# Top-k attention with a mixture of depths: moving half a mask between two rows of maxima, and one-hot slots to GpSimd at the end

## The chip, the cores and the metric

The kernel runs on one core of a Trainium2 chip. The metric is the device time in microseconds (us), the median of several executions. The core's engines run at the same time, each through its own instruction queue in order: TensorE (PE, with its weight loads as PEld), VectorE (DVE), ScalarE (ACT), GpSimd (POOL) and SyncE (SP), which only issues DMAs here. They wait for one another through semaphores.

## What is computed

Two blocks follow each other. The attention block has 8 batches, 8 heads, 576 tokens and a head size of 64. Of every row of scores the 32 largest are kept:

```python
scores = scale * np.matmul(q, k.transpose(0, 1, 3, 2))
kth = np.partition(scores, -top_k, axis=-1)[..., -top_k:-top_k + 1]
mask = scores >= kth
scores = np.where(mask, scores, -1000000000.0)
attn = softmax(scores)            # written out in the original
attn_out = np.matmul(attn, v)
```

The heads are joined to x of shape (8, 576, 512). The second block, the mixture of depths, lets only 128 tokens of each batch through a small network and adds the result to these rows:

```python
scores = np.einsum('bsd,d->bs', x, w_gate)
out = x.copy()
for b in range(B):
    top_idx = np.argpartition(-scores[b], capacity)[:capacity]
    xe = x[b, top_idx]
    ye = np.maximum(xe @ w1, 0.0) @ w2
    g = 1.0 / (1.0 + np.exp(-scores[b, top_idx]))
    out[b, top_idx] = x[b, top_idx] + g[:, None] * ye
```

## The kernel before

**Units and steps.** The scores of a batch are cut into 18 units of two tiles of 128 rows by 576 columns, 144 units in all (`units`). A software pipeline runs over them: one step `n` of the main loop works on several units at once. In step n
- TensorE turns (transposes) the scores of unit n-4 into PSUM and subtracts a large number where the mask says "less than the 32nd" (`weigh`, tiles `ptr`, `less`), multiplies the scores of unit n+1 (`multiply`, tile `ps`), and multiplies the weights of unit n-4 with v (`values`, tile `av`),
- ScalarE takes the exponential of the turned scores (`pT`, `last`), makes one tile's half of the mask of unit n-3 (`less`), copies the scores of unit n+1 out of PSUM (`sc`), copies the values (`xs`), and finds on which side of a bound the scores of unit n-1 lie (`seen`, `sides`),
- VectorE finds a bound for unit n (`find_bound`: eight maxima of 72 columns for each of the two tiles, `cand<-sc`, then three rounds of `best`), and the 32nd largest of unit n-2 (`find_kth`, `next<-y`),
- GpSimd makes the other tile's half of the mask of unit n-3 (`less`), and multiplies scores and sides of unit n-1 (`y<-sc,sides` twice, then the small `y<-steps,seen`).

**The order.** Each engine's order is the order in which the program writes its instructions; nothing rearranges them. Work that may come a little later is kept in lists: `vector_late` holds closures for VectorE, and `flush_vector` runs them. `find_bound` runs them at line 387, that is between the eight maxima of its first tile and those of its second.

**The mixture of depths** of batch b runs as a generator (`mixture`) within the next steps, a part at a time, at the steps that `mix_at` lists: gates, ranks, one-hot slots (`pick`), a matmul that gathers each slot's row number (`multiply_places`), an indirect DMA that gathers the rows (`fetch_rows`), TensorE's parts of the network (`h_ps`, eight parts, and `y_ps`, eight parts), and an indirect DMA that adds the result to the output (`add_rows`, the scatter), which GpSimd issues. In the step in which GpSimd issues a scatter it has no room for its half of the mask, and VectorE makes it: these are the six `scatter_steps`, one for each of the batches 0 to 5 (line 992, used in line 1091). There `mask_of(n - 3, (act, dve))` writes VectorE's half at the top of the step, ahead of the maxima of `find_bound`.

**The end.** Behind the last unit, `closing` (line 736) does the last batch's mixture of depths with nothing left to hide it, while the batch before has its last eight parts of y (`between`) still to do. `count` ranks the tokens; since the last 64 gates come late, the rank is the sum of a count among the first 512 (`ranks`) and one among the last 64 (`others`), and a slot's one-hot row is `slot - rank == others`. Then follow: five matmuls of `multiply_places`, the sum of the parts (`place`), the row numbers (`row_i`), the gather of `xe` by an indirect DMA, four transposes, 32 matmuls of h in four groups (`ps`, `av`, `h_ps`, `ptr`), eight of y into `ps`, one product on VectorE (`gy`), and the indirect DMA that puts the rows (`put_rows`).

Of the line numbers in the profile, L43 stands for almost everything: the helper `InOrder` records every operation there. The groups are told apart by their tiles.

Of the kernel before, what the change touches and what calls it, by code (L numbers as in the profile page):

```python
# [11 lines left out]
ALU = mybir.AluOpType  # L12
# [34 lines left out]
def kernel(  # L47
# [117 lines left out]
    def load_weights():  # L165
        sp.dma_start(
            out=wg, in_=dataclasses.replace(moe_w_gate, ap=[[0, P], [1, HD]])
        )
        sp.dma_start(out=w1, in_=moe_w1.rearrange("(c p) f -> p c f", p=P))
        sp.dma_start(out=w2, in_=moe_w2.rearrange("(c p) n -> p c n", p=P))  # L170

    pe, dve, act, pool, sp = (
        InOrder(tc, e)
        for e in (nc.tensor, nc.vector, nc.scalar, nc.gpsimd, nc.sync)
    )


    late, vector_late, pool_late = [], [], []
# [23 lines left out]
    def room_for_qkv(b):  # L202

        kT = kqpool.tile([P, NHP, R + S], FP32, name="kT")
        qT = kqpool.tile([P, NHP, S], FP32, name="qT")
        return kT, qT, vbufs[b % 2]
# [96 lines left out]
    def turn_pair(rows, hp):  # L306
        tr = ps_tr.tile([P, 2, J, P], FP32, name="ptr")
        for w in range(2):
            rows.turn(2 * hp + w, tr[:, w, :, :])
        for w in range(2):  # L310
            rows.keep(2 * hp + w, tr[:, w, :, :])
# [8 lines left out]
    def load_v(vb, vs):  # L320
        vt, vpair = vs
        v_rows = vb[:, JP:S, :].rearrange("h p d -> p h d")
        for hh in range(2):
            sp.dma_start(
                out=vpair[hh * R : (hh + 1) * R, :, hh, 0:D], in_=v_rows[:, hh::2, :]
            )
        for h in range(H):
            sp.dma_start(
                out=vt[:, h, :, 0:D],
                in_=vb[h, 0:JP, :].rearrange("(p j) d -> p j d", j=J),  # L330
            )
# [109 lines left out]

    def mask(sc, next8, on=None):

        less = wkpool.tile([P, 2, S], BF16, name="less")
        for i, engine in enumerate(on or (act, pool)):
            kth = next8[:, i, 7:8]
            if engine is act:
                act.activation(less[:, i, :], sc[:, i, :], AF.Relu, bias=kth, scale=-1.0)
            else:
                engine.tensor_scalar(  # L450
                    out=less[:, i, :],
                    in0=sc[:, i, :],
                    scalar1=kth,
                    scalar2=None,
                    op0=ALU.is_lt,
                )
        return less

    def turn_some(tr, z, less):
# [7 lines left out]
    def room_to_turn():  # L467
        return ps_tr.tile([P, 2, J, P], FP32, name="ptr"), ps_av.tile(
            [P, 512], FP32, name="av"
        )  # L470
# [62 lines left out]
    def normalise(b, t, xs):  # L533
        n = R if t == J else P
        den = sums[0:n, b * NT + t, :]
        divide(n, xs, of_batch[b][0][0:n, t, :], den)
# [199 lines left out]
    def closing(b, pg, between):  # L736
# [44 lines left out]
        yield  # L781
        spread(J, NT)
        split(*pg)
        for _ in range(3):
            next(between)
        for t in range(J):
            count(t, slice(JP, S), others)
        for t in range(J):
            dve.tensor_scalar(
                out=pick[:, t, :],  # L790
                in0=slot,
                scalar1=rank[:, t : t + 1],
                scalar2=others[:, t : t + 1],
                op0=ALU.subtract,
                op1=ALU.is_equal,
            )
        count(J, slice(0, S), rank)
        dve.tensor_scalar(
            out=pick[0:R, J, :],
            in0=slot[0:R, :],  # L800
            scalar1=rank[0:R, J:NT],
            scalar2=None,
            op0=ALU.is_equal,
# [44 lines left out]
        for fc in range(NFC):  # L848
# [6 lines left out]
            out=gy, in0=ps, scalar=g[:, 0:1], in1=xe, op0=ALU.mult, op1=ALU.add  # L855
# [15 lines left out]
    def split(gate, parts):  # L871

        rest = modpool.tile([P, NT], FP32, name="rest")
        pool.tensor_copy(out=parts[:, :, 1, 0], in_=gate)
        pool.tensor_tensor(rest, gate, parts[:, :, 1, 0], ALU.subtract)
        pool.tensor_copy(out=parts[:, :, 1, 1], in_=rest)
        pool.tensor_tensor(rest, rest, parts[:, :, 1, 1], ALU.subtract)
        pool.tensor_copy(out=parts[:, :, 1, 2], in_=rest)
# [65 lines left out]
    def gates(b, t):  # L944
        dot_tile(t, *of_batch[b])
# [42 lines left out]
    for b in range(B - 1):  # L988
# [3 lines left out]
    scatter_steps = {  # L992
        (b + 1) * per_batch + mix_at_of.get(b, mix_at)[-1] + 1 for b in range(B - 2)
    }

    place_steps = {}
    for b in range(B - 1):
        n = (b + 1) * per_batch + mix_at_of.get(b, mix_at)[6]
# [17 lines left out]
    def is_unit(n):  # L1016
        return 0 <= n < N
# [31 lines left out]
    def mask_of(n, on=None):  # L1049
        b, i = divmod(n, per_batch)  # L1050
        masks[n] = mask(scs[n], next8s[b][:, i, :, :], on)
        if i == per_batch - 1:
            at = 2 * per_batch * b
            pool.tensor_copy(
                out=seen[:, 1, at : at + 2 * per_batch].rearrange("p (n i) -> p n i", i=2),
                in_=next8s.pop(b)[:, :, :, 7],
            )

    for n in range(-1, N):
        b, i = divmod(n, per_batch)  # L1060
        if i == 0 and 0 <= b < B - 1:
            qkv[b + 1] = room_for_qkv(b + 1)
            loading = chain(
                loading, Rows(k[b + 1], q[b + 1], *qkv[b + 1][0:2]).parts()
            )
        if 0 < n + 1 < NHP:
            turn_pair(first_rows, n + 1)
        if n == 1:
            load_v(v[0], qkv[0][2])
        if n == NHP:  # L1070
            load_weights()


        gating = normalised
        if inverting is not None:
            normalised = inverting[0:2]
            vector_late.insert(0, lambda a=inverting: normalise(*a))
            inverting = None
        else:
            normalised = None  # L1080
        if gating is not None:
            vector_late.append(lambda a=gating: gates(*a))

        if is_unit(n - 4):
            tr, av = room_to_turn()
            pT, last, exp = weigh(scs.pop(n - 4), tr, av, masks.pop(n - 4))
            exp()
        if is_unit(n - 3):  # L1090
            mask_of(n - 3, (act, dve) if n in scatter_steps else None)
        flush()
        if is_unit(n + 1):
            b, t, g = units[n + 1]
            ps = room_for_scores()
            multiply(t, g, *qkv[b][0:2], ps)
            b, i = divmod(n, per_batch)
            loads = list(islice(loading, first_loads[i] if b == 0 else loads_at[i]))
            halves = [ps[:, a, :, HALF : HALF + P] for a in range(2)]
            for load, half in zip(loads, halves):  # L1100
                load[0](half)
            scs[n + 1] = keep(ps)
            for load, half in zip(loads, halves):
                load[1](half)
        if is_unit(n - 4):
            b4, t4, g4 = units[n - 4]
            values(t4, g4, pT, last, av, qkv[b4][2])
            if n in place_steps:
                values_bank[0] = av
                next(mixtures[place_steps[n]])  # L1110
            if g4 == 0:
                xs = xpool.tile([P, H, DE], FP32, name="xs")
                if t4 == 0:
                    x = xpool.tile([P, NT, HD], FP32, name="x")
                    pg = gates_of[b4 % 2]
                    of_batch[b4] = x, pg
            keep_values(t4, g4, av, xs)
            if g4 == groups(t4) - 1:
                inverting = b4, t4, xs
                n4 = R if t4 == J else P  # L1120
                keep_sums(n4, xs, sums[0:n4, b4 * NT + t4, :])
            while kept:
                kept.pop(0)()


        if is_unit(n):
            bests[n] = find_bound(scs[n])
        flush_vector()
        flush_pool()
        if is_unit(n - 2):  # L1130
            kth_of(n - 2)
        while after_kth:
            after_kth.pop(0)()


        if is_unit(n - 1):
            what_is_below(n - 1)

        if gating is not None:
            b, t = gating  # L1140
            if t == J:
                store(out[b], of_batch[b][0])
                mixtures[b] = mixture(float(b * S), of_batch[b][1], ranks[:, b, :])
        for b in mix_steps.get(n, ()):
            next(mixtures[b], None)
        b, i = divmod(n, per_batch)
        if i == v_at and 0 <= b < B - 1:
            load_v(v[b + 1], qkv[b + 1][2])
# [72 lines left out]
    for what, op, than, limit in (  # L1221
# [10 lines left out]
            out=sure, in0=far, scalar=limit, in1=sure, op0=than, op1=ALU.mult  # L1232
# [134 lines left out]
```

## Time and profile before

The time before is 854.24 us, the median of 3 runs (853.79 to 854.92). The profiled execution took 852.91 us and spans 851.1 us.

| engine | busy us | share of the span | instructions |
|---|---|---|---|
| PE | 791.2 | 93% | 9839 |
| DVE | 806.8 | 95% | 4904 |
| ACT | 761.2 | 89% | 1704 |
| POOL | 727.5 | 85% | 727 |

All four engines are busy nearly all of the time up to about 800 us. A step takes about 5.5 us. The last 50 us are different: one chain after another of short instructions, in which engines wait for each other. A busy time includes whatever an instruction spends on waiting inside itself, for a port for example, so a high share alone doesn't say which engine sets the pace. A matmul's end is modelled, so that TensorE's shares are rather too high.

### The profile page before, as it was taken

To read this page: it belongs to the slowest core of one execution; us is meant where nothing else is said; L and a number is where in the kernel's file an instruction comes from. 1 tells how busy PE (TensorE), PEld (TensorE's weight loads), DVE (VectorE), ACT (ScalarE), POOL (GpSimd) and SP (SyncE) were. 2 spreads that over 40 slices of the span, in tenths; PEclk is the share of its full clock that TensorE was granted. 3 is DMA by queue.
4 is the path that set the end of the run, shared out by engine and by line. 5 is a ranking of instruction groups with operands and counts; after the bars stand their busy time and mean duration, and the time that the engine had idled before them with its cause. 6 is when DMAs were issued, how large, how long until landed. Compare 5 with 4: busy or idle time off the path is not lost. (4 is left out here: it accounts for less than half of the span.)

```text
span 851.1 us, 28068 instructions
## 1 busy us (share of the span) xinstructions
PE 791.2 (93%) x9839; PEld 610.5 (72%) x9839; DVE 806.8 (95%) x4904; ACT 761.2 (89%) x1704; POOL 727.5 (85%) x727
## 2 busy tenths in 40 slices
PE   5798889988999999999999999999999999999977
PEld 4566667666777778877787777877787777777845
DVE  5999999999999999999999999999999999999960
ACT  4899999999999999999999999999999999989830
POOL 3799889999989989999899999999898998988820
PEclk9899999999999999999999999999999999999998
DMA  9931112321141221511233221412215102101021
GB/s 173 277 71 31 36 64 39 90 50 29 57 96 27 51 39 57 109 40 39 76 54 75 48 44 57 97 27 52 39 57 109 27 6 72 22 15 15 2 70 28
DMA packets 122133, 50.37 MB, mean 59 GB/s; under 512 B 116416, under 2 KB 116416, under 8 KB 120960
## 3 DMA queue, kind: packets, MB, share of 16 engines
q1 hardware_dynamic: 118672, 43.91, 21.5%
q0 software_dynamic: 1728, 4.20, 2.7%
q8 instruction: 79, 1.29, 0.7%
q14 instruction: 70, 0.57, 0.3%
q10 hardware_dynamic: 1584, 0.39, 0.2%
HBM read 36.93 MB, written 11.55 MB: 57 GB/s over the span
## 5 line engine op out<-in xcount | busy, mean ns | idle before, releaser
L43 POOL TENSOR_TENSOR y<-sc,sides 128x576 f32<-128x576 f32 x288 | 365.4, 1290 | 76.8 <-ACT sides L43 74.1
L43 DVE MAX8 cand<-sc 128x8 f32<-128x72 f32 x2304 | 330.3, 216 | 8.4 <-ACT sc L43 8.4
L43 POOL TENSOR_SCALAR less<-sc,next 128x576 bf16<-128x576 f32 x135 | 232.8, 1724 | 5.2 <-DVE next L43 4.5
L43 ACT ACTIVATE sides<-sc,seen 128x576 bf16<-128x576 f32 x288 | 221.0, 768 | 5.2
L43 PE MATMUL ptr<-out_of_reach,less 128*128 128x128 bf16 x1136 | 204.1, 220 | 17.3 <-POOL less L43 17.2
L43 PE MATMUL ptr<-ident,sc 128*128 128x128 f32 x1136 | 213.7, 279 | 0.0
L43 DVE MAX8 next<-y 128x8 f32<-128x584 f32 x288 | 204.4, 751 | 2.2 <-POOL y L43 2.0
L43 PE MATMUL ps<-kT,qT 64*128 64x288 f32 (+1 forms) x1280 | 181.0, 430 | 7.2 <-ACT qT L43 5.3
L43 PEld LDWEIGHTS av<-v,pT 128*64 128x64 f32 x4544 | 144.1, 137 | 49.0 <-ACT last L43 36.6
L43 PE MATMUL av<-v,pT 128*64 128x65 f32 x4544 | 163.8, 224 | 16.4 <-ACT last L43 15.2
L43 PEld LDWEIGHTS ptr<-ident,sc 128*128 128x128 f32 x1136 | 160.4, 141 | 22.3 <-PE av L43 8.7
L43 ACT COPY sc<-ps 128x1152 f32<-128x1152 f32 x144 | 161.0, 1118 | 8.9 <-PE ps L43 7.6
L43 PEld LDWEIGHTS <-less 128*128 128x128 bf16 x1296 | 133.0, 103 | 37.6 <-POOL less L43 23.3
L43 ACT ACTIVATE pT<-ptr 128x1024 f32<-128x1024 f32 x142 | 144.2, 1015 | 16.2 <-PE ptr L43 13.5
L43 DVE MAX8 best<-cand 128x8 f32<-128x24 f32 (+2 forms) x864 | 141.8, 200 | 0.6 <-DVE cand L43 0.6
L43 PEld LDWEIGHTS ps<-kT,qT 64*128 64x128 f32 (+1 forms) x1280 | 98.1, 177 | 45.8 <-issue 21.9
L43 ACT ACTIVATE less<-sc,next 128x576 bf16<-128x576 f32 x143 | 110.6, 774 | 8.9 <-DVE next L43 8.7
L43 DVE MATCH_REPLACE8 cand<-best,cand 128x24 f32<-128x24 f32 (+1 forms) x576 | 101.9, 185 | 0.0
L43 PE MATMUL av<-vpair,last 128*128 128x130 f32 (+1 forms) x314 | 68.1, 317 | 0.0
L43 PE MATMUL h_ps<-xeT,w 128*128 128x128 f32 x464 | 61.9, 278 | 0.2 <-ACT xeT L43 0.2
L43 PEld LDWEIGHTS h_ps<-xeT,w 128*128 128x128 f32 x464 | 56.0, 192 | 2.5 <-ACT xeT L43 1.3
L43 PE MATMUL y_ps<-w,hT 128*128 128x512 f32 x112 | 56.7, 601 | 0.0
(124 smaller groups left out, 865.2 us busy)
## 6 DMA issues: line engine op xcount, KB each, us to landing
v<-in_v_dram SPq DMA_DIRECT2D x64, 128.0 KB, 3.3
out_dram<-x SPq DMA_DIRECT2D x8, 1024.0 KB, 3.9
rows<-in_k_dram SPq DMA_DIRECT2D x56, 128.0 KB, 3.7
rows<-in_q_dram SPq DMA_DIRECT2D x56, 128.0 KB, 3.3
w<-in_moe_w_dram SPq DMA_DIRECT2D x2, 2048.0 KB
gate_row<-row_dram SPq DMA_DIRECT2D x7, 288.0 KB, 4.2
w<-in_k_dram SPq DMA_DIRECT2D x8, 128.0 KB
last<-in_k_dram SPq DMA_DIRECT2D x8, 128.0 KB, 3.1
```

The source lines that it names most:

```text
L43: return lambda *a, **kw: self._tc.keep_in_program_order(fn(*a, **kw))
```

## The change

Two things are changed.

1. In the six scatter steps VectorE's half of the mask is no longer written at the top of the step. `mask` puts it at the head of `vector_late`, and so it runs in `find_bound` between the eight maxima of the first tile and those of the second.
2. In `closing`, three of the four full tiles of one-hot slots that were made by VectorE are made by GpSimd, and one more part of the earlier batch's y is left for the time behind `multiply_places`, in which the gather is under way: two parts come before it and four after it (three and three before the change). The first two of the eight parts come earlier, and are the same in both.

```diff
         for i, engine in enumerate(on or (act, pool)):
             kth = next8[:, i, 7:8]
             if engine is act:
                 act.activation(less[:, i, :], sc[:, i, :], AF.Relu, bias=kth, scale=-1.0)
             else:
-                engine.tensor_scalar(
-                    out=less[:, i, :],
-                    in0=sc[:, i, :],
-                    scalar1=kth,
-                    scalar2=None,
-                    op0=ALU.is_lt,
-                )
+
+                def is_less(engine=engine, i=i, kth=kth):
+                    (engine or dve).tensor_scalar(
+                        out=less[:, i, :],
+                        in0=sc[:, i, :],
+                        scalar1=kth,
+                        scalar2=None,
+                        op0=ALU.is_lt,
+                    )
+
+                if engine:
+                    is_less()
+                else:
+                    vector_late.insert(0, is_less)
         return less
...
-        for _ in range(3):
+        for _ in range(2):
             next(between)
         for t in range(J):
             count(t, slice(JP, S), others)
         for t in range(J):
-            dve.tensor_scalar(
+            (pool if t < 3 else dve).tensor_scalar(
                 out=pick[:, t, :],
                 in0=slot,
                 scalar1=rank[:, t : t + 1],
...
         if is_unit(n - 3):
-            mask_of(n - 3, (act, dve) if n in scatter_steps else None)
+            mask_of(n - 3, (act, None) if n in scatter_steps else None)
```

The first part is there because VectorE's mask and GpSimd's products meet in that step; the second shortens what VectorE has to do before the gather of the end, and gives TensorE more to do while the gather runs.

## The prediction

> **What bounds the kernel now.** I first cut the span into stages with the view of busy time by stretch (columns: stretch, its length, busy time and instructions of PE, PEld, DVE, ACT and POOL, then the granted TensorE clock, the DMA share and GB/s).
>
> ```profile
> 302.00:324.00 22.00, 19.98 (x274) 16.35 (x272) 21.89 (x127) 21.04 (x50) 19.80 (x19) 1.00 0.32 86
> 324.00:401.00 77.00, 76.98 (x958) 58.88 (x957) 76.89 (x483) 74.06 (x167) 71.06 (x70) 1.00 0.24 51
> 401.00:423.00 22.00, 19.97 (x274) 16.34 (x272) 21.89 (x126) 21.04 (x48) 19.73 (x20) 1.00 0.32 85
> ```
>
> A batch takes 99.2 us (its scatter steps begin at 304.1 and 403.3). VectorE has hardly any idle time in either stretch (0.11 us). TensorE has none in the 77 us, and 2.0 us in the 22 us around a scatter. So two chains are tight: VectorE by itself, and TensorE with ScalarE. Next I read the timeline around one scatter, engine by engine (start, us, engine, instruction, idle time before it and its releaser).
>
> ```profile
> 303.17 2.52 POOL L43 TENSOR_TENSOR y<-sc,sides 128x576 f32<-128x576 f32 x2
> 305.64 0.44 POOL L43 TENSOR_TENSOR y<-steps,seen 128x16 f32<-128x16 f32 x1
> 306.42 1.63 POOL L43 DMA_INDIRECT out_dram<-gy,row_i  x1 [0.34 <-DVE less L43]
> ...
> 304.09 1.92 DVE L43 TENSOR_SCALAR less<-sc,next 128x576 bf16<-128x576 f32 x1
> 305.94 2.24 DVE L43 MAX8 cand<-sc 128x8 f32<-128x72 f32 x16
> ...
> 310.29 0.78 ACT L43 ACTIVATE less<-sc,next 128x576 bf16<-128x576 f32 x1 [0.49 <-DVE next L43]
> ...
> 309.85 1.15 PE L43 MATMUL av<-v,pT 128*64 128x65 f32 x32 [0.64 <-ACT last L43]
> 315.96 1.15 PE L43 MATMUL av<-v,pT 128*64 128x65 f32 x32 [0.97 <-ACT last L43]
> ```
>
> ```profile
> 809.87 0.52 DVE L43 TENSOR_SCALAR less<-sc,next 128x576 bf16<-128x576 f32 x1
> ```
>
> The same mask takes 0.52 us at 809.87, beside an almost idle GpSimd, and 1.92 us here. It starts 0.92 us into GpSimd's two products and ends 0.3 us behind them: it stands still while they run. Behind it, `next` of this step is late, and ScalarE waits 0.49 us for that.
>
> Last, the end, from the timeline of TensorE and VectorE and from the instructions of `pick` (ns: least, median, most).
>
> ```profile
> 823.15 0.28 DVE L43 TENSOR_SCALAR pick<-slot,ranks 64x128 bf16<-64x128 f32 x1
> ...
> 823.49 0.17 PE L43 MATMUL av<-parts,pick 64*128 64x6 bf16 x1 [0.81 <-DVE pick L43]
> 823.59 2.84 PE L43 MATMUL y_ps<-w,hT 128*128 128x512 f32 x6
> 827.92 0.63 PE L43 MATMUL ptr<-ident,xe 128*128 128x128 f32 x4 [1.49 <-DMA xe<-out_dram,row_i]
> 829.23 2.86 PE L43 MATMUL ps<-xeT,w 128*128 128x128 f32 x16 [0.56 <-ACT xeT L43]
> 831.88 2.81 PE L43 MATMUL av<-xeT,w 128*128 128x128 f32 x16
> 834.53 1.95 PE L43 MATMUL h_ps<-xeT,w 128*128 128x128 f32 x16
> ```
>
> ```profile
> L43 POOL TENSOR_SCALAR pick<-slot,ranks x28: 599/611/622, 163.8 to 751.9; 128x128 bf16<-128x128 f32 x21, 64x128 bf16<-64x128 f32 x7
> L43 DVE TENSOR_SCALAR pick<-slot,ranks,others x4: 342/343/343, 821.3 to 822.1; 128x128 bf16<-128x128 f32 x4
> ```
>
> The chain is: last `pick` on VectorE, matmul, row numbers, gather, transposes, h. The first two groups of h take 2.8 us, the third 1.95 us for the same work: by the view of stretches the granted clock is 0.50 from about 830.3 to 833.7 us and 1.00 elsewhere.
>
> **What the Trainium skill says.** *SBUF — State Buffer*, section "SBUF: two separate sides": VectorE and GpSimd share a pair of ports as an exclusive lock; a VectorE instruction in a 2-port mode or GpSimd holds it, and the other blocks. The trace agrees (1.92 against 0.52 us), and shows more: the mask didn't get in between the two products. *VectorE: DVE Perf Modes*, section "The perf-mode tier table": a fp32 `tensor_scalar` from SBUF runs at 2x. The durations agree for one operation: between 128 and 576 columns (277 and 508 ns in the trace) a column costs 0.52 ns. The two-operation `pick` takes 342 ns, more than the 277 of one operation, so I take it as running at half that speed, and thus without the lock. *TensorE: Matmul & The Clock Gate*, Part 1: a free-running window of 3.41 us, after a quiet one the clock is halved. The trace agrees: 3.4 us at 0.50.
>
> **Part 1, the masks.** GpSimd's order doesn't change. VectorE does eight maxima first. Sixteen take 2.24 us, so eight take about 1.08 to the next start; the mask is then ready at 304.09 + 1.0 = 305.1, still ahead of the point where it was let in (306.01 - 0.52 = 305.49). It ends at about 306.0 as before, and only eight maxima are left in place of sixteen: VectorE is 1.08 us ahead. The eight maxima take the place of waiting. Behind the mask stand the second tile's maxima, which nobody is waiting for at once; TensorE wants this half at about 311.7, 5.7 us later; GpSimd's scatter sees the mask end when it did. Five of the six masks are alike (1.92 to 1.97 us). The sixth starts at 766.13 and takes 0.81 us; 1.0 later it would meet the scatter's issue, of 1.62 us, which can begin at about 766.9. If nothing blocks it, it ends at 767.6 with eight maxima fewer to do, 0.4 us won; if it stands for the whole issue, it ends at 769.0, and 1.0 us is lost. VectorE has by then a lead, so I count 0.
>
> What is the lead worth? VectorE alone: 5 x 1.08 = 5.4 us, the upper end. The other chain: in the 22 us of a scatter, TensorE's wait of 0.64 us is for ScalarE, busy without a break since 303.1; it stays. The 0.49 us that ScalarE waits for VectorE goes, and with it that much of the 0.97 us in which TensorE waits for ScalarE. From 316 us on TensorE is full for the rest of the batch. So a batch is 0.5 us shorter: 5 x 0.5 = 2.5 us. The rest of the lead, 0.58 us each time, collects as slack on VectorE, for which the scores lie ready 2.4 us or more ahead in most steps. In the last batches ScalarE waits again for VectorE (1.28 us at 754.7, 0.47 at 760.2), and TensorE then 0.76 for ScalarE at 771.2; the slack takes away about 0.6 of that. Part 1: 2.5 + 0.6 = 3.1 us.
>
> **Part 2, the slots.** VectorE loses three instructions of 0.26 us start to start (1.11 for four): its last `pick` is due at 823.15 - 0.77 = 822.38. GpSimd is free at 820.81 (the end of `split`). Before doesn't show it at a `pick` of two operations; at least it costs 0.61 us (one operation), and at most I take 0.9. VectorE's own ratio, 342 to 277, gives 0.75; I take 0.70. Three end at 820.88 + 2.1 = 822.98. VectorE's last `pick` has one operation and so wants the lock: let in 0.2 us before GpSimd's end as the mask was, at 822.78, it ends at 823.06, 0.37 us before 823.43. The gather follows this, so 0.4 us are won (0.6 with 0.61 us, 0.2 lost with 0.9). TensorE does two parts of y before, and idles a little for the slots.
>
> The fourth part behind the slots is 0.86 us (two matmuls of 0.43 start to start). From 823.66 to 827.92 TensorE waits for the gather, 4.26 us; four parts take 2.84 + 0.86 = 3.70, so the part costs nothing, and the gap falls from 1.49 to about 0.6 us. Then comes the clock. The quiet window before was 826.85 to 830.27: 1.07 + 0.56 = 1.63 us idle. The window from 816.6 to 820.0 has 1.53 us idle (from 818.06 to 819.59) and was followed by a full clock. With 0.6 + 0.56 = 1.2 us no window is as quiet as that, so I expect the full clock. Two groups of h then take 3.57 us in place of 5.30 start to start: 1.7 us won. Sum: 3.1 + 0.4 + 1.7 = 5.2 us, 854.2 - 5.2 = **849.0 us**.
>
> **The rivals.**
> - *VectorE is the only bound*: then its lead counts whole, 5.4 + 0.4 + 1.7 = 7.5 us, 846.7 us. For it: no idle time on VectorE in a batch. Against it: none on TensorE in 77 us of it either.
> - *The clock drops all the same*, or the timed runs of before didn't have it low, since the window runs free: 3.1 + 0.4 = 3.5 us, 850.7 us; with only the 0.5 us per scatter and nothing from the slots, 851.7.
> - *Slower*: the mask, coming later, misses its turn, and waits through the small product and the scatter's issue. 306.08 + 1.63 + 0.5 = 308.2 in place of 306.0, less the 1.08 won: 1.1 us lost six times, less 1.7 from the clock: about 859 us. Against it: the mask is waiting 0.4 us before its turn in five of six steps. A weaker form is the slots on GpSimd holding the last `pick` back and the sixth mask held (0.2 + 1.0 lost), with the clock low as before and less than half of the 2.5 us won: about 854, no change.
>
> **How the numbers follow.** My forecast 0.5; VectorE alone 0.2; no clock 0.2; no change or slower 0.1, about half of it each. The range takes the first three with the ends of the unknown costs: 846.2 (846.7 less 0.2 for cheaper slots and 0.3 of the sixth mask's 0.4) to 851.9 (851.7 and 0.2 for dearer slots). Faster by over 0.2% means below 852.5: 0.90; within 0.2%: 0.05; slower: 0.05.
>
> **What would show it.** Right: five masks of about 0.9 us in place of 1.92, with eight maxima ahead of each; no wait of ScalarE's `less` for `next` behind a scatter; the distance from scatter to scatter 0.5 us shorter (1.1 for the first rival); the first two groups of h near 1.95 us at a clock of 1.00; the gap before `ptr<-ident,xe` near 0.6. Wrong: masks that still take 1.9 us; a `pick` on GpSimd over 0.85 us, or VectorE's last `pick` stretched beyond 0.7; a clock of 0.50 within the last 25 us before the final y.

## The result, and the profile after

The changed kernel takes 848.55 us, the median of 6 runs (845.32 to 849.89); the kernel before, run beside it, 853.64 (6 runs, 852.79 to 854.92). The ratio is 0.9933, with an interval from 0.9913 to 0.9954. The forecast was 849.0 us. The profiled executions span 851.1 and 847.1 us. From the page after, each engine's busy time:

```profile
PE 791.5 (93%) x9839; PEld 609.8 (72%) x9839; DVE 803.8 (95%) x4901; ACT 760.2 (90%) x1704; POOL 729.4 (86%) x730
```

VectorE's busy time is 3.0 us shorter. The three slots that left it are 1.0 of that (3 x 342 ns); its other work is the same, so it stands 2 us less inside its instructions. The view of stretches around the first scatter, with the columns of before:

```profile
300.00:322.00 22.00, 20.66 (x272) 16.39 (x268) 22.00 (x137) 21.54 (x51) 20.30 (x20) 1.00 0.23 50
322.00:398.00 76.00, 75.84 (x958) 58.66 (x957) 75.89 (x469) 73.02 (x166) 70.02 (x69) 1.00 0.29 62
```

TensorE now idles 1.34 us around the scatter, where it idled 2.0, and 0.16 us in the rest of the batch. VectorE is still full. The timeline of that scatter step, engine by engine:

```profile
305.27 1.16 DVE L43 MAX8 cand<-sc 128x8 f32<-128x72 f32 x8
306.35 1.04 DVE L43 TENSOR_SCALAR less<-sc,next 128x576 bf16<-128x576 f32 x1
307.30 1.16 DVE L43 MAX8 cand<-sc 128x8 f32<-128x72 f32 x8
...
304.53 2.53 POOL L43 TENSOR_TENSOR y<-sc,sides 128x576 f32<-128x576 f32 x2
...
307.76 1.63 POOL L43 DMA_INDIRECT out_dram<-gy,row_i  x1 [0.31 <-DVE less L43]
...
311.07 0.77 ACT L43 ACTIVATE less<-sc,next 128x576 bf16<-128x576 f32 x1
...
311.22 1.15 PE L43 MATMUL av<-v,pT 128*64 128x65 f32 x32 [0.64 <-ACT last L43]
...
316.73 1.15 PE L43 MATMUL av<-v,pT 128*64 128x65 f32 x32 [0.70 <-ACT last L43]
```

The mask now begins 1.82 us into GpSimd's products, where it began 0.92 us in, and takes 1.04 us in place of 1.92. Its end, 307.39, is still 0.3 us behind the end of the products. ScalarE's own half of the mask starts with no wait for `next` (0.49 us before), and TensorE's second wait fell from 0.97 to 0.70 us. One more wait has gone. In the kernel before, GpSimd's half of the mask waited for the late `next` too, and TensorE for that half; neither wait stands in the changed kernel. From the timelines of the kernel before:

```profile
311.12 1.73 POOL L43 TENSOR_SCALAR less<-sc,next 128x576 bf16<-128x576 f32 x1 [0.32 <-DVE next L43]
...
312.90 0.23 PE L43 MATMUL ptr<-out_of_reach,less 128*128 128x128 bf16 x1 [0.25 <-POOL less L43]
```

Added up from one scatter to the next, TensorE's waits are shorter by 0.68, 0.54, 0.43, 0.21 and 0.89 us. The distances between the scatters are shorter by nearly the same: 0.62, 0.57, 0.49, 0.08 and 0.89 us.

The end, from the timeline of TensorE, the instructions of `pick` (ns: least, median, most) and VectorE's timeline:

```profile
820.75 0.18 PE L43 MATMUL av<-parts,pick 128*128 128x6 bf16 x1 [0.65 <-POOL pick L43]
821.53 0.31 PE L43 MATMUL av<-parts,pick 128*128 128x6 bf16 x3 [0.60 <-POOL pick L43]
821.77 3.70 PE L43 MATMUL y_ps<-w,hT 128*128 128x512 f32 x8
826.07 0.63 PE L43 MATMUL ptr<-ident,xe 128*128 128x128 f32 x4 [0.60 <-DMA xe<-out_dram,row_i]
...
827.38 2.05 PE L43 MATMUL ps<-xeT,w 128*128 128x128 f32 x16 [0.56 <-ACT xeT L43]
829.26 1.95 PE L43 MATMUL av<-xeT,w 128*128 128x128 f32 x16
```

```profile
L43 POOL TENSOR_SCALAR pick<-slot,ranks,others x3: 788/805/828, 819.1 to 820.7; 128x128 bf16<-128x128 f32 x3
...
820.79 0.40 DVE L43 TENSOR_SCALAR pick<-slot,ranks 64x128 bf16<-64x128 f32 x1
```

A group of h is eight matmuls of the program, with two records for each. The fourth part of y lies inside the wait for the gather, the gap before the transposes is 0.60 us (1.49 before), and both first groups of h run at full speed (2.86 and 2.81 us before). The slots on GpSimd cost 0.8 us each, and TensorE waits for two of them.

To see where the time went, I cut the span of every profiled run at the same instructions: VectorE's first maximum of unit 18 and of unit 143 (the last), the start of the last transpose of gates, and the end. All six scatters lie in the second column, and the column "scatters" gives the time from the first scatter's issue to the sixth's within it. The column "start" varies with how long the clock is halved in the first 40 us, which none of these kernels touches (last section). Us:

| kernel | start | unit 18 to 143 | scatters | unit 143 to gate | gate to end |
|---|---|---|---|---|---|
| before | 107.31 | 690.27 | 460.75 | 22.01 | 31.48 |
| changed | 109.03 | 686.37 | 458.10 | 22.47 | 29.25 |
| e1: masks moved, end as before | 112.27 | 685.43 | 458.09 | 22.50 | 31.70 |
| e2: mask in place, times a constant | 111.24 | 688.90 | 460.04 | 22.02 | 30.09 |
| e3: only the fourth part of y | 110.88 | 688.86 | 460.81 | 22.00 | 30.09 |
| e4: only the slots | 109.46 | 688.94 | 460.29 | 22.03 | 29.51 |
| e5: mask in place, times a column | 112.85 | 689.64 | 460.57 | 22.00 | 31.65 |
| e6: changed, half of h | 108.95 | 681.49 | 455.12 | 21.10 | 26.14 |
| e7: masks moved, two slots | 109.16 | 685.90 | 457.47 | 22.44 | 29.22 |
| e8: changed, all of y ahead | 109.71 | 685.41 | 457.29 | 22.49 | 33.82 |
| e9: mask in place, counting | 110.78 | 684.71 | 457.22 | 22.49 | 31.30 |

The five kernels with the plain mask at the top, or a two-operation one (before, e2 to e5), lie at 688.86 to 690.27 (mean 689.3) from unit 18 to 143, the four with the mask between the maxima and all of h (changed, e1, e7, e8) at 685.41 to 686.37 (mean 685.8). The ranges don't meet. Each kernel has one profile here, so the size is rougher than these figures look: by the means the masks are worth 3.5 us there, and 0.46 of that is lost again just behind.

### The profile page after: what moved, and what is told of

Read it like the earlier page. It is cut to its first block, busy times and chain, and to the rows that moved or that the text cites. A ratio compares the mean times of both kernels' runs of the same rounds, so it can differ in the third digit from the quotient of the medians.

```text
span 847.1 us, 28068 instructions
## 1 busy us (share of the span) xinstructions
PE 791.5 (93%) x9839; PEld 609.8 (72%) x9839; DVE 803.8 (95%) x4901; ACT 760.2 (90%) x1704; POOL 729.4 (86%) x730
```

## The experiments

The theory: the mask stood for ports that GpSimd's products held (a), what it cost reached the time through ScalarE and TensorE and not through VectorE alone (b), and in the end the quiet gap halved the clock (c). Rivals: the mask stood for its data or a buffer; VectorE is the only bound; the slots on GpSimd, not the y part, shorten the end.

**e1: the masks alone.**

```diff
+                    vector_late.insert(0, is_less)
...
-            mask_of(n - 3, (act, dve) if n in scatter_steps else None)
+            mask_of(n - 3, (act, None) if n in scatter_steps else None)
```

> Only the masks are moved; slots and y as before. Theory (a lead of VectorE counts only as far as ScalarE waited for it): the distance from one scatter's mask to the next falls from 99.2 us to about 98.6, about 3 us in all up to the last unit, and the end is as before, with the first two groups of h slow in about every second execution: about 850.6 us. Rival (VectorE alone sets the pace): 98.1 us from mask to mask, about 848.2 us.

Measured: 849.83 us (16 runs) against 853.44 (27 runs), ratio 0.9954 with an interval from 0.9939 to 0.9969. Two masks took 0.50 us, having come behind GpSimd's products, and the others about 1.08. The clock was low for 3.41 us in the end, the first groups of h took 3.28 and 2.40 us, and the gap was 1.50. So the masks alone give 3.6 us of the 5.1 that the change gives. The time doesn't tell the theory from the rival, since the interval is 848.2 to 850.8 us; the first three distances from scatter to scatter, 99.05, 98.78 and 98.52 us, lie nearer to the theory's 98.6 than to the rival's 98.1. Nor does time show that the end adds anything to the masks: the intervals of e1 and of the change overlap (0.9939 to 0.9969, 0.9913 to 0.9954).

**e2 and e5: the mask left at the top, with a second operation.** If a two-operation form ran without VectorE's fast mode, it wouldn't need GpSimd's ports and would pass at about 0.8 us. The second operation multiplies by one, as a constant in e2 and as a column in e5. The masks of the last two units keep the plain form.

```diff
+                twice = engine is dve and on == (act, dve)
...
-                    scalar2=None,
+                    scalar2=1.0 if twice else None,
...
+                    **(dict(op1=ALU.mult) if twice else {}),
```

> As before, with the mask at the top of the scatter's step, but as an instruction of two operations (less than, then times 1.0)[...]. Theory (the mask stood for the shared ports): it takes about 0.81 us in place of 1.92 although GpSimd's products are under way, GpSimd's small product behind them takes 0.21 in place of 0.44 us, and from mask to mask it is 98.6 us. Rival (the mask waits for something else, data or a buffer): it still ends at 0.3 us behind the products, 1.9 us long.

The edit of e5 differs in the operand:

```diff
+    one = const.tile([P, 1], FP32, name="one")
+    nc.gpsimd.memset(one, 1.0)
...
+                    scalar2=one if twice else None,
```

> As before, with the mask at the top of the scatter's step, as an instruction of two operations whose second number, 1.0, also comes from a column in SBUF, the form of the slots that took 342 ns. Theory (the mask stood for the shared ports, and this form doesn't use the second port): about 0.81 us in each of the six scatter steps, GpSimd's small product behind it 0.21 in place of 0.44 us, and from mask to mask about 98.6 us. Rival (it waits for data or a buffer): 1.9 us as in the run with a constant 1.0.

In both it was the rival that came out. From VectorE's timelines, e2 first:

```profile
406.76 1.96 DVE L43 TENSOR_SCALAR less<-sc,next 128x576 bf16<-128x576 f32 x1
```

```profile
408.23 1.94 DVE L43 TENSOR_SCALAR less<-sc,next,one 128x576 bf16<-128x576 f32 x1
```

In the first five steps both masks stand as long as before (1.92 to 1.96 us), the scatters are as far apart as before (460.04 and 460.57 us from first to sixth), and the times, of one execution each, are 854.12 and 857.92 us. So a second operation doesn't avoid the wait, and these two runs couldn't tell the ports from the data as the cause.

**e9: the mask left at the top, in the form that counts as it compares.** A third form settles it: with `accum_out` the same instruction also sums its output (into a column that nobody reads).

```diff
+                counts = {}
+                if engine is dve and on == (act, dve):
+                    many = stats.tile([P, 1], FP32, name="many")
+                    counts = dict(op1=ALU.add, accum_out=many)
...
+                    **counts,
```

> As before, with the mask at the top of the scatter's step, but in the form of the ranks' counts, which also adds up its results: in the trace of before 44 counts take at most 0.81 us at 576 columns, however busy GpSimd is. Theory (the plain mask stands for ports shared with GpSimd, and this form doesn't use them): 0.80 us and a read of the sum of 0.08 in all six scatter steps, GpSimd's small product behind it 0.21 in place of 0.44 us, and 98.6 us from mask to mask. Rival (it waits for data or a buffer, which are the same here): 1.9 us again.

From the timelines of VectorE and GpSimd in e9:

```profile
405.67 0.81 DVE L43 TENSOR_SCALAR_CACHE_REDUCE less<-sc,next 128x576 bf16<-128x576 f32 x1
406.41 0.08 DVE L43 DVE_READ_ACCUMULATOR less<-sc,next 128x1 f32 x1
...
404.75 2.53 POOL L43 TENSOR_TENSOR y<-sc,sides 128x576 f32<-128x576 f32 x2
407.24 0.21 POOL L43 TENSOR_TENSOR y<-steps,seen 128x16 f32<-128x16 f32 x1
```

In the second to fifth step the mask begins 0.92 us into GpSimd's products, as in the kernel before (in the first it begins 2.28 us in, in the sixth 2.15). It reads the same scores and bound, writes the same tile, and takes 0.81 us in all six steps. GpSimd's small product behind it takes 0.21 us in place of 0.44. Data, buffers and place are unchanged and only the form of the instruction differs. So the plain mask stood for something that GpSimd's products hold and the counting form doesn't need. That is shown; the rival of data and buffers falls. The forecast of 98.6 us from mask to mask came out too: from first to sixth scatter e9 takes 457.22 us, at least as short as the change (458.10), without moving anything. Its 851.06 us is a single run, with the clock low in the end, beside 853.34 for the kernel before.

**e6: the changed kernel with half of h's products left out**, so that TensorE has less to do while VectorE's and GpSimd's instructions stay.

```diff
-        for dc in range(NDC):
+        for dc in range(NDC // 2):
...
-                stop=(dc == NDC - 1),
+                stop=(dc == NDC // 2 - 1),
```

> The changed kernel with half of every product of h left out (two of four chunks of the inner dimension), which takes some 3.7 us of matmuls a batch off TensorE and nothing off the other engines. Theory (behind a scatter TensorE and ScalarE set the pace, and VectorE stands in its dot product with the gate weights for GpSimd, with 0.4 us to spare): from mask to mask 0.4 to 1 us shorter than 98.6, no more since VectorE then is next, and that dot product back near 1.1 us or less. Rival (VectorE alone sets the pace): 98.6 us as in the changed kernel.

It took 839.97 us. The view of stretches, and one mask from VectorE's timeline:

```profile
322.00:398.00 76.00, 74.57 (x936) 56.23 (x932) 75.89 (x477) 72.69 (x167) 70.03 (x71) 1.00 0.25 53
```

```profile
403.44 0.50 DVE L43 TENSOR_SCALAR less<-sc,next 128x576 bf16<-128x576 f32 x1
```

TensorE idles 1.43 us in 76 now (0.16 in the changed kernel), and a batch takes 97.6 to 98.1 us in place of 98.6 to 98.8 in three of the changed kernel's four. VectorE's work is the same, and it is as full as ever (75.89 us): what has gone is its standing inside the mask (0.50 against 1.07 us) and inside the next dot product `prod` (1.26 against 1.53, where 1.1 or less was forecast), 0.85 us together. So VectorE's fullness contains waiting for GpSimd, whose pace the other engines set, and "VectorE is the only bound" falls as a reading of the 95%. VectorE follows closely behind, though: half of h's products bring only 0.8 us a batch.

**e3, e4 and e8: the end.** Masks as before in all but e8. In e3 only the fourth part of y moves; in e4 only the slots; in e8, which is the changed kernel otherwise, all six parts of y come ahead of the slots, so that TensorE has nothing to do amid the gather.

```diff
-        for _ in range(3):
+        for _ in range(2):
```

> Only the fourth part of y behind the slots; masks and slots as before. Theory (the quiet window halves the clock): TensorE's gap before the transposes of xe is about 0.6 us in place of 1.49, the clock is 1.00 throughout the last groups of h, and these take 1.95 us each; from the slots' last matmul to the last y 1.7 us less than before, about 852.2 us. Rival (the low clock has another cause, such as its time since the last change): the first two groups take 2.8 us all the same, and the time is that of before.

```diff
-            dve.tensor_scalar(
+            (pool if t < 3 else dve).tensor_scalar(
```

> Only three slots by GpSimd; masks as before, three parts of y before and three behind. By the changed kernel's trace GpSimd's three slots take 2.40 us, so the last matmul of the slots comes 0.1 us earlier than before, counted from the last gate; the gap before the transposes stays near 1.5 us. Rival (VectorE's three instructions less count whole): 0.8 us earlier.

```diff
-        for _ in range(2):
-            next(between)
+        for _ in range(6):
+            next(between, None)
```

> The changed kernel with all six last parts of y ahead of the slots and none amid the gather. Theory: the last matmul of the slots comes about 1.6 us later, TensorE's gap before the transposes is about 4.2 us, a window is quiet in every phase, and the first groups of h run at a clock of 0.50 for 3.4 us, so that h takes 1.6 us longer than in the changed kernel, together about 3.3 us. Rival (the low clock has nothing to do with the gap): h takes 7.2 us as there.

e3 took 853.06 us (12 runs), ratio 1.0007 with an interval from 0.9988 to 1.0026: no gain in time. Its trace looks as the theory has it: gap 0.60, no halved clock, h groups of 2.05 and 1.95 us. From the gate to the end it takes 30.09 us, though, and so does e2, which has the end of the kernel before and happened to keep the full clock. So the part of y by itself gains nothing there; only the clock can. e4 took 851.77 us. TensorE's timeline of e4, then of e8:

```profile
828.71 0.63 PE L43 MATMUL ptr<-ident,xe 128*128 128x128 f32 x4 [1.54 <-DMA xe<-out_dram,row_i]
...
830.01 2.05 PE L43 MATMUL ps<-xeT,w 128*128 128x128 f32 x16 [0.56 <-ACT xeT L43]
```

```profile
827.72 1.09 PE L43 MATMUL ptr<-ident,xe 128*128 128x128 f32 x4 [4.33 <-DMA xe<-out_dram,row_i]
...
829.48 3.78 PE L43 MATMUL ps<-xeT,w 128*128 128x128 f32 x16 [0.56 <-ACT xeT L43]
```

In e4 the last matmul of the slots ends 3.97 us behind the last transpose of gates, in place of 4.08: the slots gain 0.11 us. And a gap of 1.54 us was followed by a full clock, while 1.49 in the kernel before was followed by a halved one. In e8 a gap of 4.33 us was followed by a halved clock for 6.83 us, two windows where one was forecast, and the four transposes too ran at half speed. From the gate to the end it takes 33.82 us, 4.6 more than the changed kernel, where 3.3 were forecast.

Over all profiles: with a gap near 1.5 us the clock was halved in four of six (before, e1, e5, e9; not in e2 and e4). With 0.6 to 0.7 it was halved in none of four (changed, e3, e6, e7). With 4.3 it was (e8). These are eleven executions, one of each kernel.

**e7: a version meant to beat both**, the changed kernel with two slots on GpSimd in place of three, and a two-operation mask.

```diff
-            (pool if t < 3 else dve).tensor_scalar(
+            (pool if t < 2 else dve).tensor_scalar(
...
+                        scalar2=None if engine else one,
...
+                        **({} if engine else dict(op1=ALU.mult)),
```

> The changed kernel with the mask in the form of two operations and two columns, between the maxima, and two slots by GpSimd in place of three. Theory: from mask to mask 98.6 us as in the changed kernel, since VectorE's further lead isn't what counts; the last matmul of the slots 0.4 to 0.5 us earlier than in the changed kernel (3.97 us behind the last gate there); about 848.1 us. Rival (VectorE alone): another 0.25 us in each of five batches, about 847 us. If the mask still stands for GpSimd: as the changed kernel.

It took 849.06 us (6 runs) against 854.47 (11 runs), ratio 0.9937 with an interval from 0.9924 to 0.9950: not to be told from the change's 0.9933. TensorE's timeline:

```profile
820.88 0.18 PE L43 MATMUL av<-parts,pick 64*128 64x6 bf16 x1 [0.23 <-DVE pick L43]
```

The masks took 1.04 to 1.07 us in the first five steps, as in the changed kernel. The last matmul of the slots ends 3.56 us behind the gate, 0.40 sooner than in the changed kernel, since GpSimd's third slot no longer comes last. Four tenths of a microsecond are below what these runs can tell.

## Why the prediction was right, and where it was not

**The masks: 3.1 us forecast, 3.5 less 0.46 measured.** The mechanism is in the main the one forecast: five masks of about 1.05 us, as many maxima ahead of them, no wait of ScalarE for `next`, and a TensorE wait of 0.64 us that stays. The way from there to TensorE was only half right. Of the 0.49 us that ScalarE no longer waits, the forecast let all pass on to TensorE; 0.27 did. Another 0.25 us came through GpSimd's half of the mask, a wait that the forecast left out. The first term, 0.5 us per scatter, held in sum: 2.65 us over the five distances, against 2.5. Three of them are about 98.7 us in place of 99.2. The fourth gained least, 99.87 against 99.95; the trace shows there a wait of ScalarE before it copies into `xs`, 0.54 us longer than before, for something that it names only as remote. In e8, with the same masks, that distance is 98.87 us, so the move of the masks doesn't by itself cause this. The fifth, of 63.08 us, gained 0.89.

The second term, 0.6 us in the last batches, came out near zero in sum: 0.85 us are won between the sixth scatter and unit 143 (29.55 against 30.40), and 0.46 are lost at once behind it, because an ordinary mask at 800.9 now meets GpSimd and stands 1.55 us in place of 0.57. Every profile with a faster batch, but for e6, shows that loss (the fourth column: 22.44 to 22.50 against 22.00 to 22.03). The sixth mask was a case of its own as feared, but harmless: 0.50 us, beside a scatter's issue that took 1.78 us in place of 1.62.

**The step that failed: "the rest of the lead, 0.58 us each time, collects as slack on VectorE".** It doesn't. In the step after the scatter VectorE's dot product `prod` now comes earlier, and stands longer, for GpSimd's products:

```profile
420.69 1.53 DVE L43 CUSTOM_DVE_ANT_0 prod<-x,wg 128x512 f32<-128x512 f32 x1
...
419.14 2.53 POOL L43 TENSOR_TENSOR y<-sc,sides 128x576 f32<-128x576 f32 x2
```

It took 1.09 us in the kernel before, where it began 1.98 us into these products; now it begins 1.55 us in and takes 1.53. In both it ends 0.55 us behind the products. So a part of the lead is given back at the next meeting with GpSimd: 1.08 us won, 0.44 lost, 0.64 left, which is close to what a batch gained. Whether a `prod` without this wait would free more wasn't tried.

**The slots: 0.4 us forecast, 0.11 measured.** The step that failed is the price of 0.70 us of a two-operation `pick` on GpSimd: 0.79 to 0.83. Then the last of GpSimd's slots, and not VectorE's last one, sets the end, and the forecast's hold of that one until GpSimd ends was wrong too: it took 0.40 us while GpSimd's ran beside it, 0.28 alone. That a two-operation form runs at half speed *and so without the lock* was my own step. I took it from the 342 ns; *VectorE: DVE Perf Modes*, "The perf-mode tier table", in the Trainium skill gives the 2x of a fp32 `tensor_scalar` and doesn't speak of a second operation. The step is refuted by e2 and e5: a two-operation mask stands for GpSimd like a plain one. The half speed is refuted by e7, whose sixth mask came behind GpSimd's products:

```profile
765.27 0.56 DVE L43 TENSOR_SCALAR less<-sc,next,one 128x576 bf16<-128x576 f32 x1
```

One operation took 0.50 us in the changed kernel's sixth mask. So the second operation adds about 0.06 us at 576 columns, and as much at 128 (342 ns, against 277 for a tile of 64 rows). It doesn't double the time of a column. The lock itself, from *SBUF — State Buffer*, "SBUF: two separate sides", agrees with e9, 0.81 against 1.92 us; that it is ports which GpSimd holds is the page's statement, and the runs show only that it holds something.

**The fourth part of y: nothing forecast, nothing measured.** The gap was forecast at about 0.6 and is 0.60 us.

**The clock: 1.7 us forecast, at most about 1.1 on average.** Between these two profiles the time from h's start to y is 1.63 us shorter, as forecast. But the term was counted whole, as if every execution of the kernel before had the clock halved, and by the profiles it is so in four of six: 1.6 x 4/6 = 1.1 us. That average is an estimate from few profiles, and e3, which isolates it, showed no gain in 12 runs (its interval reaches 0.12%, 1.0 us, on the side of faster). So the size of this term is open between nothing and about 1.1 us. That the drop goes with a long gap fits the counts above (none of four, four of six, one of one), which are few.

**The sum.** 3.5 - 0.46 for the masks, 0.1 for the slots and nothing to 1.1 for the clock make 3.1 to 4.2 us, against 5.1 between the medians (3.9 to 7.4 us by the ratio's interval). What the rest is stays open. Two of the changed kernel's six executions, the fastest (845.32 and 846.41 us), also have the highest mean clock (0.994 and 0.996 against 0.990 to 0.992), so a part of it may be a start with less of the halved clock. That the forecast of 5.2 came so near is therefore in part luck: the slots and the clock were counted too high, and about as much stands in the measurement without an explanation.

## What to carry to other kernels

An instruction that stands for something another engine holds showed the wait here in its duration (1.92 against 0.52 us) and not as idle time. Compare the same shape beside a busy and beside an idle neighbour; then move it behind work that has to be done anyway, or look for a form that isn't held (0.81 us in e9). Expect part of the lead to go at the next place where the two engines meet; find that place in the trace before counting the lead. A gain that rests on a free-running clock window counts by the share of executions in which the window falls badly, and one profile of before shows only whether it fell so once.

## What was not expected of the hardware

- The counting form of the mask was never held by GpSimd's products (0.81 us in six of six steps), while one and two operations without the sum were (1.92 to 1.97 us in five of six).
- GpSimd's two products of 576 columns (2.53 us together) didn't let a plain mask in between them, but its slots, which read one tile, hardly held VectorE's: in the changed kernel a one-operation slot on VectorE that began 0.1 us into one of GpSimd's, of 0.79 us, took 0.40 us (0.28 alone) and ended well before it.
- One gap alone doesn't decide the clock's fall. TensorE's idle time in the whole 3.41-us window ahead orders the cases better: the first fall of the end came behind windows with 1.62 (before), 1.86 (e9), 2.03 (e5), 2.06 (e1) and 3.35 us idle (e8), and windows with 1.52 to 1.60 us had none behind them, except in e8, where one with 1.53 us kept the clock low. Between the two the order is lost, since windows with 1.68 (e4) and 1.74 us (e1) had no fall behind them either. Matmul ends are modelled, so these figures can't tell whether there is a sharp threshold. *TensorE: Matmul & The Clock Gate*, Part 1, describes the free-running window; no run here shows what decides in it.
- The clock is also halved near the start, for 6.8 us in one execution and 13.65 in another of the profiled ones. From the view of stretches, before and then changed (the clock is the third number from the end):

```profile
31.00:37.00 6.00, 4.55 (x60) 3.37 (x58) 5.35 (x35) 5.60 (x11) 6.00 (x7) 0.95 1.04 393
```

```profile
31.00:37.00 6.00, 4.93 (x26) 3.27 (x26) 5.36 (x36) 4.95 (x10) 6.00 (x7) 0.50 1.04 395
```

  It makes a part of the "start" column, 107.3 to 112.9 us, and is likely the largest share of the spread of one kernel's runs (849.96 to 856.12 us in 27 runs of the kernel before). In these 27, the three with a mean clock of 0.995 or 0.996 are the three fastest (849.96 to 850.44 us), and the 15 with 0.990 or less take 852.13 to 856.12. Another 11 runs, with 0.988 to 0.993, show no such order. The mean doesn't say where in a run the clock was low, and no run tested this by itself.
